# Wide row-sum products, transposes by DMA and a new instruction order in a fused attention and rational-activation MLP kernel

## The chip, the cores and the metric

The kernel runs on one core of a Trainium2 chip. The metric is the device time of one execution in microseconds (us). Times are medians of several runs. Every group of runs also holds runs of the kernel before on the same chip, and a ratio below is the mean time of a kernel's fast runs over the mean time of the fast runs of before in the same rounds, so it is not quite the ratio of the two medians. The interval beside it is a 95% interval. A run more than 1.5% above the fastest run of its kernel counts as slow and is left out of the ratios; the medians and ranges are of all runs. Each profile is of one single run.

## The reference

```
scores = (q @ k^T) / sqrt(64)                  # q, k, v: 8 batches, 8 heads, 576 positions, 64
mask:  heads 0-3: 0 <= i-j < 32                 # local
       heads 4-7: i >= j and i%32 == j%32       # strided
x = softmax(masked scores) @ v                  # rearranged to 4608 x 512
h = x @ w_in                                    # 512 -> 2048
g = (a0 + a1 h + a2 h^2 + a3 h^3) / (1 + |b0||h| + |b1| h^2 + 1e-6)
out = g @ w_out                                 # 2048 -> 512
```

## The kernel before

The work of one batch is attention in five tiles (0 to 3 hold 512 of the positions, tile 4 the remaining 64) and then a chunk of 512 rows of the MLP. Attention of later batches runs between the dense products of earlier chunks. The program is a list of operations, each a group of instructions of one engine with its dependencies, and a list `ORDER` gives each operation its rank in its engine's stream. An operation that has to wait therefore holds up everything behind it on the same engine.

The softmax denominators come from TensorE: each block of 32 columns of exponentials (`ES`, `EW`) is loaded as weights and multiplied once by the values and once more by a column of ones. `psA` is the accumulator; its column 64 in each group of 128 is the denominator.

```python
# attend(), tiles 0-3: strided heads
for h in range(4):
    for g in range(4):
        gh, j = divmod(g, 2); u = 2 * h + gh
        w = ES[es][64*c:64*c+64, j, 64*u+32*sh : 64*u+32*sh+32]           # 64 x 32 weights
        mm(pa4[32*g:32*g+32, 1, h, 0:64],  w, VT[iv][64*c:64*c+64, h, 64*g:64*g+64])
        mm(pa4[32*g:32*g+32, 1, h, 64:65], w, ONE[64*c:64*c+64, :])       # row sums
# tile 4: the same with EW, 128 x 32 weights
...
# VectorE: RC = 1 / psA[.., 64];  XR = psA[.., 0:64] * RC
# SyncE:   XT = DMA transpose of XR  (feeds the first dense product, psH <- XT, Win)
```

Other parts that matter here:

```python
TB, NF0 = 8, 70
# queries and keys of the strided heads, batches b < TB: TensorE transposes into PSUM, VectorE copies to sT
# first-layer weight Win: 4 loads of 0.5 MB early on;  second-layer weight, one load of 2 MB:
def load_wout(key, dep):                       # issued by GpSimd after the loads of batch 2's turn
    add("POOL", lambda e: e.dma_start(Wout[:, :, :], w_out.rearrange("(f p) o -> p f o", p=128)), ...)
# first values: one VectorE, one ScalarE (1.91 us) and one GpSimd (2.6 us) copy into VL
# warm-up: NF0 filler products of 128 columns
```

The softmax here doesn't subtract the row's maximum and nothing guards it: scores larger than these inputs give would overflow.

Of the kernel before, what the change touches and what calls it, by code (L numbers as in the profile page):

```python
# [4 lines left out]
dt = mybir.dt  # L5
Alu = mybir.AluOpType
AF = mybir.ActivationFunctionType
BF = dt.bfloat16
# [7 lines left out]
def _bf16_bits(x):  # L16
# [7 lines left out]
    0, 2, 1, 19, 3, 127, 71, 72, 73, 116, 33, 86, 99, 156, 153, 83, 110, 78, 105, 114, 34, 17, 98, 101, 109,  # L24
    12, 103, 36, 140, 82, 53, 108, 117, 97, 61, 25, 43, 118, 100, 50, 18, 112, 26, 60, 48, 29, 87, 55, 32,
    52, 23, 11, 104, 49, 51, 22, 30, 85, 35, 41, 56, 28, 84, 107, 59, 57, 44, 94, 81, 37, 119, 10, 62, 31,
    115, 111, 21, 141, 42, 15, 46, 45, 14, 40, 66, 79, 4, 27, 6, 58, 7, 68, 5, 38, 9, 13, 16, 8, 20, 24, 92,
    91, 93, 102, 77, 90, 132, 139, 65, 54, 39, 122, 47, 126, 63, 69, 70, 113, 75, 160, 158, 147, 154, 157,
    159, 67, 76, 74, 80, 64, 89, 88, 96, 95, 106, 123, 130, 131, 133, 136, 120, 124, 125, 143, 146, 135,
    142, 144, 148, 151, 129, 134, 138, 145, 150, 152, 170, 173, 178, 197, 207, 216, 221, 240, 121, 137, 162,  # L30
    164, 171, 194, 184, 202, 188, 179, 182, 198, 191, 175, 208, 149, 128, 204, 236, 239, 215, 211, 301, 299,
    229, 303, 193, 206, 228, 234, 225, 237, 238, 242, 243, 245, 161, 168, 174, 181, 183, 192, 200, 186, 190,
    195, 196, 203, 210, 155, 163, 165, 166, 169, 213, 232, 172, 176, 189, 217, 231, 241, 177, 187, 167, 180,
    201, 214, 223, 249, 256, 227, 235, 244, 246, 254, 283, 199, 209, 185, 205, 219, 226, 212, 220, 233, 250,
    292, 357, 375, 312, 341, 300, 307, 315, 322, 393, 398, 252, 258, 260, 263, 272, 255, 262, 264, 269, 273,
    265, 270, 274, 278, 280, 257, 268, 277, 281, 285, 230, 267, 275, 302, 287, 324, 333, 337, 343, 224, 222,
    251, 253, 261, 259, 282, 286, 290, 266, 271, 247, 276, 248, 294, 291, 279, 218, 318, 319, 306, 311, 313,
    320, 316, 296, 460, 284, 289, 293, 298, 304, 310, 314, 323, 327, 334, 309, 339, 345, 350, 355, 342, 347,
    348, 354, 353, 359, 360, 363, 365, 369, 370, 374, 373, 376, 378, 380, 381, 389, 390, 400, 288, 295, 297,
    305, 331, 335, 340, 382, 402, 351, 362, 372, 383, 386, 414, 308, 326, 317, 329, 406, 434, 438, 459, 479,  # L40
    448, 468, 494, 498, 514, 518, 330, 371, 356, 366, 377, 388, 384, 395, 410, 418, 426, 436, 503, 472, 521,
    442, 457, 483, 488, 501, 536, 325, 321, 328, 361, 336, 344, 346, 352, 349, 332, 338, 358, 364, 368, 392,
    396, 385, 387, 425, 427, 403, 405, 435, 409, 445, 415, 367, 379, 391, 397, 404, 412, 420, 429, 439, 444,
    394, 421, 451, 466, 464, 449, 452, 453, 458, 461, 463, 465, 469, 470, 473, 475, 478, 477, 480, 482, 484,
    485, 534, 548, 578, 407, 416, 399, 408, 424, 432, 413, 422, 441, 454, 431, 447, 462, 489, 456, 467, 507,
    523, 527, 567, 581, 552, 558, 543, 551, 574, 587, 612, 624, 535, 554, 557, 563, 580, 593, 603, 634, 541,
    549, 555, 559, 562, 615, 597, 599, 608, 568, 576, 590, 598, 604, 701, 669, 703, 670, 411, 428, 401, 455,
    417, 430, 437, 446, 443, 423, 419, 440, 433, 450, 491, 495, 487, 493, 547, 550, 505, 502, 513, 510, 515,
    544, 471, 476, 481, 486, 490, 492, 497, 500, 504, 509, 474, 496, 512, 516, 519, 564, 570, 571, 573, 575,
    577, 579, 611, 583, 589, 591, 594, 595, 600, 601, 605, 606, 655, 660, 693, 506, 511, 517, 528, 532, 546,  # L50
    525, 531, 553, 556, 561, 565, 585, 592, 538, 560, 613, 621, 627, 674, 677, 654, 702, 640, 645, 688, 729,
    713, 734, 635, 656, 663, 675, 694, 709, 717, 744, 609, 618, 628, 643, 662, 672, 762, 691, 668, 667, 679,
    705, 719, 725, 791, 761, 765, 790, 499, 508, 533, 530, 545, 539, 524, 526, 529, 537, 522, 542, 520, 540,
    626, 620, 617, 629, 651, 653, 614, 610, 647, 642, 657, 641, 566, 572, 584, 586, 588, 596, 602, 607, 616,
    619, 582, 623, 625, 630, 632, 676, 681, 683, 686, 687, 690, 692, 697, 698, 706, 708, 721, 711, 715, 716,
    718, 723, 742, 776, 795, 633, 646, 650, 665, 673, 682, 638, 648, 689, 696, 700, 710, 714, 720, 658, 671,
    724, 732, 737, 803, 814, 788, 810, 752, 758, 775, 825, 830, 838, 750, 769, 778, 797, 807, 827, 832, 856,
    730, 740, 755, 764, 785, 789, 802, 823, 826, 793, 813, 821, 831, 835, 839, 899, 842, 907, 569, 637, 631,
    652, 622, 666, 684, 644, 636, 659, 639, 661, 649, 664, 731, 733, 735, 728, 759, 757, 738, 739, 766, 743,
    774, 771, 678, 685, 695, 699, 704, 707, 712, 722, 727, 745, 726, 749, 753, 770, 772, 784, 792, 794, 798,  # L60
    799, 804, 805, 808, 812, 815, 816, 819, 818, 822, 824, 828, 837, 872, 873, 876, 736, 741, 747, 767, 773,
    781, 780, 796, 786, 800, 806, 820, 829, 833, 801, 809, 836, 844, 848, 888, 912, 879, 901, 864, 866, 921,
    929, 933, 942, 862, 875, 880, 892, 913, 925, 930, 946, 846, 858, 870, 877, 886, 904, 905, 900, 898, 889,
    897, 928, 931, 939, 962, 966, 943, 963, 779, 680, 783, 787, 751, 782, 754, 760, 777, 746, 748, 768, 763,
    756, 852, 847, 841, 843, 874, 868, 855, 850, 861, 857, 863, 859, 811, 817, 834, 845, 851, 854, 867, 878,
    881, 883, 869, 884, 887, 895, 910, 885, 890, 891, 893, 894, 902, 903, 916, 906, 909, 911, 914, 918, 922,
    923, 926, 964, 983, 985, 994, 840, 849, 853, 860, 865, 871, 915, 919, 882, 896, 908, 917, 920, 927, 924,
    932, 935, 938, 941, 965, 974, 953, 976, 949, 951, 968, 998, 993, 1002, 947, 954, 957, 969, 973, 979,
    986, 1006, 944, 948, 950, 952, 958, 992, 991, 997, 961, 970, 972, 977, 980, 984, 1015, 987, 1012, 988,
    934, 937, 940, 945, 955, 960, 936, 956, 967, 971, 975, 978, 982, 990, 959, 981, 995, 1000, 1001, 1034,  # L70
    1043, 1020, 1039, 1013, 1017, 1051, 1060, 1026, 1037, 1007, 1021, 1023, 1030, 1036, 1041, 1046, 1067,
    989, 996, 999, 1003, 1005, 1011, 1014, 1009, 1008, 1016, 1019, 1022, 1025, 1028, 1054, 1029, 1033, 1056,
    1004, 1018, 1027, 1032, 1042, 1045, 1010, 1024, 1050, 1055, 1058, 1074, 1085, 1081, 1095, 1062, 1064,
    1080, 1091, 1096, 1100, 1048, 1059, 1065, 1071, 1076, 1082, 1084, 1099, 1110, 1087, 1088, 1105, 1108,
    1112, 1121, 1089, 1093, 1098, 1103, 1104, 1106, 1119, 1113, 1116, 1118, 1130, 1143, 1145, 1035, 1047,
    1094, 1127, 1133, 1137, 1142, 1136, 1139, 1141, 1146, 1148, 1150, 1031, 1038, 1040, 1044, 1049, 1053,
    1073, 1072, 1075, 1052, 1057, 1061, 1063, 1066, 1068, 1077, 1079, 1069, 1070, 1078, 1083, 1086, 1090,
    1124, 1123, 1135, 1126, 1092, 1097, 1101, 1102, 1115, 1132, 1131, 1128, 1120, 1107, 1109, 1111, 1114,
    1117, 1122, 1125, 1129, 1134, 1138, 1140, 1144, 1147, 1149, 1151, 1152, 1153, 1159, 1157, 1156, 1155,
    1154, 1158, 1160, 1162, 1161  # L80
# [203 lines left out]
def bass_strided_sparse_attn__then__act_rational_pade_kernel(nc, q, k, v, moe_w_in, moe_w_out, moe_a, moe_b, out):  # L284
    w_in, w_out, pa, pb = moe_w_in, moe_w_out, moe_a, moe_b
    B, H, S, D = q.shape
# [10 lines left out]
    HL, DA, TB, NF0 = 4, 1, 8, 70  # L297
# [18 lines left out]
    ES = [A(f"ES{i}", [128, 2, 512], BF) for i in range(NE)]  # L316
    EL = [A(f"EL{i}", [128, 2, 512], BF) for i in range(NE)]
    EX = [A(f"EX{i}", [128, 2, 64], BF) for i in range(NE)]
    EW = [A(f"EW{i}", [128, 12, 2, 32], BF) for i in range(NE)]
# [72 lines left out]
    def cload(name, dst_t, arr, key):  # L392
        g = chan(name).group()
        c = const(name + "_v", arr)
        return add("SP", (lambda e: e.dma_start(dst_t.bitcast(dt.uint16)[:, :], c[:, :])), [], 0.1, key, g, 0.1)
# [6 lines left out]
    cst_c = nc.inline_tensor(cst_np, name="c_cst")  # L402
    cons = []
    cons.append(add("SP", lambda e: e.dma_start(
        cst[:, :], bass.AP(tensor=cst_c, offset=0, ap=[[0, 128], [1, 2]])), [], 0.1, -500, gC, 0.1))
    cons.append(add("SP", lambda e: e.dma_start(
        coef[:, 0:4], bass.AP(tensor=pa.tensor, offset=pa.offset, ap=[[0, 128], [1, 4]])), [], 0.1, -500, gC, 0.1))
    cons.append(add("SP", lambda e: e.dma_start(
# [740 lines left out]
```

## Time and profile before

Before the change the kernel takes 382.73 us (median of 3; 382.16 to 1815.88, the last being the very first execution). The profiled execution has a span of 381.5 us.

In the profiles PE and PEld are TensorE's products and weight loads, DVE is VectorE, ACT ScalarE, POOL GpSimd and SP SyncE. "Issue" is time in which an engine waited for nothing that the profile shows. The granted clock is the share of TensorE's full clock that the chip allowed.

The profile page of before: the span, each engine's busy time with its share and its instructions, TensorE's busy tenths and its granted clock in tenths over 40 equal slices, and the chain of waits followed back from the end, by engine and by line.

```profile
span 381.5 us, 10809 instructions
PE 335.1 (88%) x4902; PEld 178.3 (47%) x4902; DVE 320.0 (84%) x280; ACT 286.9 (75%) x234; POOL 136.0 (36%) x193
PE   4859948989983699999999999999999999999940
PEclk9967975999996699999999999999999999999995
PE 74%; DMA 8%; DVE 7%; issue 4%; ACT 3%; SPq 1%; DVEq 0%
```

The row of tenths shows two halves. Up to slice 14 (about 128 us) TensorE has holes, and its clock is at times halved; after that it reads 9 until the last two slices. The clock matters for time: eight 128x512 products take 3.42 us where it is halved and 1.73 us elsewhere. The table by stretches (start:end, length, then busy us and instructions of PE, PEld, DVE, ACT and POOL, then granted clock, DMA share, GB/s) says the same in numbers.

```profile
100.00:120.00 20.00, 15.50 (x451) 9.40 (x449) 18.27 (x20) 14.81 (x14) 9.18 (x13) 0.95 1.09 129
120.00:140.00 20.00, 13.67 (x199) 6.55 (x198) 14.32 (x12) 12.78 (x12) 16.75 (x24) 0.71 1.33 161
140.00:200.00 60.00, 60.00 (x944) 30.64 (x942) 56.38 (x39) 53.43 (x42) 19.27 (x25) 1.00 0.60 85
```

The worst hole, at 113 to 128 us, seems to have an owner. The first lines below are the view of the tile `Wout` (its load by GpSimd is issued at 107.3 us and takes 19.0 us to land); the last is from the chain of waits in order of time (start, length, what).

```profile
L460 POOL DMA_DIRECT2D Wout<-in_moe_w_out_dram x1: 1180/1180/1180, 107.3 to 107.3; - x1
DMA to landing us min/median/max: 19.0/19.0/19.0
115.75 12.59 DMA XT<-XR
```

A transpose of 128 KB that the next dense chunk needs takes 12.6 us to land while the weight is being loaded (the median of all such transposes in this trace is 4.1 us). The weight lands at 107.3 + 19.0 = 126.3 us, the transpose at 128.3, and the dense chunk starts at 128.4 us. The view of waits puts only 2.1 us of TensorE's own idle time here directly on `XT`, more on "issue" (3.0) and on other engines.

How cheap are the row sums? The groups by form for tile `psA` list duration of one matmul in ns (min/median/max), the first and last start, and the shape of the array piece.

```profile
L597 PE MATMUL psA<-ONE,ES x432: 161/164/188, 21.2 to 261.8; 64*32 64x1 bf16 x144
L597 PE MATMUL psA<-VT,ES x416: 186/197/239, 21.1 to 261.8; 64*32 64x64 bf16 x139
```

Each is 0.16 to 0.20 us from start to end, but products on different 64x32 pieces of the array overlap, as the timeline of one tile shows (start, length of the stretch, what, count; lines left out at the dots):

```profile
161.49 0.24 PE L597 MATMUL psA<-VL,EL 64*32 64x65 bf16 x8
161.54 0.20 PE L597 MATMUL psA<-VT,ES 64*32 64x64 bf16 x1
...
161.62 0.16 PE L597 MATMUL psA<-ONE,ES 64*32 64x1 bf16 x1
161.63 0.20 PE L597 MATMUL psA<-VT,ES 64*32 64x64 bf16 x2
161.64 0.16 PE L597 MATMUL psA<-ONE,ES 64*32 64x1 bf16 x1
...
161.84 0.20 PE L597 MATMUL psA<-ONE,ES 64*32 64x1 bf16 x3
161.97 1.90 PE L597 MATMUL psO<-Wout,T 128*128 128x512 bf16 x8
```

A whole tile of 48 matmuls takes 161.97 - 161.49 = 0.48 us (tile 4: 0.88 us). The 48 start within 0.38 us of each other, 8 ns apart on average (single ones 1 to 28 ns); the last 0.10 us is the change to the next shape. A duration in the list above is a latency, not a cost.

### The profile page before, as it was taken

The page shows a single profiled execution, that of the slowest core. Times are in us where ns is not written, and L with a number is a line of the kernel's source. Part 1 is how long each engine was busy: PE and PEld are TensorE (multiplying, and loading weights), DVE is VectorE, ACT ScalarE, POOL GpSimd, SP SyncE. Part 2 cuts the span into 40 slices and gives each one's busy share as a digit, 9 for nine tenths or more (in the row PEclk, how much of TensorE's full clock was granted, in tenths as well). Part 3 has the DMA queues.
Part 4 walks back from the last instruction along what each step waited for, and adds up shares of the span by engine and source line. Part 5 has one row for each costly group of instructions (what it writes and reads, how often), then busy time and mean ns, then how long its engine had stood idle before and what let it go on. Part 6 is the DMA issues. An engine that isn't in the chain of part 4 may idle for free.

```text
span 381.5 us, 10809 instructions
## 1 busy us (share of the span) xinstructions
PE 335.1 (88%) x4902; PEld 178.3 (47%) x4902; DVE 320.0 (84%) x280; ACT 286.9 (75%) x234; POOL 136.0 (36%) x193
## 2 busy tenths in 40 slices
PE   4859948989983699999999999999999999999940
PEld 4734536554452345554555455454444455544410
DVE  0545995979989588899999999999999999999930
ACT  2423891889983598979889999799998899877710
POOL 0893898706934930069308802600000000000000
PEclk9967975999996699999999999999999999999995
DMA  6999999849999960689839694915020331140412
GB/s 206 194 183 166 94 151 99 96 68 85 153 109 179 173 83 2 77 115 127 140 81 93 110 142 88 106 25 125 15 47 9 76 82 29 41 97 1 103 30 87
DMA packets 80254, 37.10 MB, mean 97 GB/s; under 512 B 49360, under 2 KB 75152, under 8 KB 80208
## 3 DMA queue, kind: packets, MB, share of 16 engines
q0 software_dynamic: 48576, 16.79, 41.1%
q1 hardware_dynamic: 31632, 19.62, 24.8%
q8 instruction: 38, 0.62, 0.7%
q14 instruction: 8, 0.07, 0.1%
HBM read 36.90 MB, written 9.44 MB: 121 GB/s over the span
## 4 chain that ended last, share of the span: by engine, by line
PE 74%; DMA 8%; DVE 7%; issue 4%; ACT 3%; SPq 1%; DVEq 0%
PE psO L597 33%; PE psH L597 21%; PE psS L597 10%; PE psA L597 7%; DMA XT<-XR 3%; DMA XW<-XR 2%; DMA HB<-in_k_dram 2%; PE psS L600 2%; DVE XR L855 2%; DVE UU L976 1%; DVE T L1002 1%; ACT HB L947 1%; DVE UU L973 1%; DVE T L961 1%; DVE T L1012 1%
## 5 line engine op out<-in xcount | busy, mean ns | idle before, releaser
L597 PE MATMUL psO<-Wout,T 128*128 128x512 bf16 x512 | 116.8, 379 | 0.0
L597 PE MATMUL psH<-XT,Win 128*128 128x512 bf16 x336 | 82.2, 387 | 2.6 <-DMA XT<-XR 2.1
L985 ACT ACTIVATE UU<-UU,cst 128x2048 bf16<-128x2048 bf16 (+1 forms) x38 | 72.3, 1910 | 4.4 <-DVE UU L976 4.4
L597 PEld LDWEIGHTS psO<-Wout,T 128*128 128x128 bf16 x512 | 48.8, 98 | 55.8
L988 ACT ACTIVATE UU<-UU 128x2048 bf16<-128x2048 bf16 (+1 forms) x38 | 68.5, 1819 | 0.1
L947 ACT ACTIVATE HB<-psH 128x1024 bf16<-128x1024 f32 x48 | 49.1, 1023 | 20.4 <-PE psH L597 20.1
L597 PEld LDWEIGHTS psH<-XT,Win 128*128 128x128 bf16 x336 | 31.3, 99 | 40.7 <-issue 3.7
L1012 DVE TENSOR_TENSOR T<-T,UU 128x4096 bf16<-128x4096 bf16 (+2 forms) x23 | 41.9, 1821 | 6.0 <-ACT UU L988 5.5
L499 POOL DMA_DIRECT2D VL<-in_v_dram x24 | 24.1, 1010 | 55.8 <-PE psA L597 55.8
L976 DVE TENSOR_TENSOR UU<-UU,T 128x4096 bf16<-128x4096 bf16 (+2 forms) x23 | 42.0, 1827 | 0.6
L1002 DVE TENSOR_TENSOR T<-T,HB 128x8192 bf16<-128x8192 bf16 (+3 forms) x17 | 41.0, 2412 | 0.3
L1006 DVE TENSOR_TENSOR T<-T,HB 128x8192 bf16<-128x8192 bf16 (+3 forms) x17 | 41.0, 2412 | 0.3
L961 DVE TENSOR_SCALAR T<-HB 128x8192 uint16<-128x8192 uint16 (+3 forms) x17 | 22.1, 1305 | 5.4 <-ACT HB L947 4.3
L973 DVE TENSOR_SCALAR UU<-T,coef 128x4096 bf16<-128x4096 bf16 (+2 forms) x23 | 25.8, 1122 | 0.7
L597 PE MATMUL psO<-XT,Win 128*128 128x512 bf16 x96 | 24.4, 399 | 1.0 <-DVE XT L608 0.5
L855 DVE TENSOR_TENSOR XR<-psA,RC 128x512 bf16<-128x512 f32 (+1 forms) x35 | 22.0, 630 | 2.1 <-DMA XW<-XR 0.8
L1009 DVE TENSOR_SCALAR T<-T,coef 128x8192 bf16<-128x8192 bf16 (+3 forms) x17 | 23.2, 1367 | 0.2
L478 POOL DMA_DIRECT2D tm<-in_k_dram x32 | 20.3, 638 | 8.6 <-DMA HB<-in_q_dram 8.6
L1004 DVE TENSOR_SCALAR T<-T,coef 128x8192 bf16<-128x8192 bf16 (+3 forms) x17 | 22.9, 1345 | 0.3
L995 ACT ACTIVATE T<-HB,coef 128x4096 bf16<-128x4096 bf16 x6 | 22.8, 3794 | 0.0
L1078 ACT ACTIVATE OS<-psO 128x1024 f32<-128x1024 f32 x16 | 16.5, 1030 | 8.0 <-PE psO L597 7.9
L478 POOL DMA_DIRECT2D tm<-in_q_dram x32 | 22.1, 695 | 0.3 <-DMA LT<-tm 0.3
(165 smaller groups left out, 501.3 us busy)
## 6 DMA issues: line engine op xcount, KB each, us to landing
out_dram<-OS SPq DMA_DIRECT2D x72, 128.0 KB
kn<-in_k_dram POOLq DMA_DIRECT2D x14, 256.0 KB, 5.7
qn<-in_q_dram POOLq DMA_DIRECT2D x14, 256.0 KB, 5.3
Win<-in_moe_w_in_dram POOLq DMA_DIRECT2D x4, 512.0 KB, 7.6
Wout<-in_moe_w_out_dram POOLq DMA_DIRECT2D x1, 2048.0 KB, 19.0
VL<-in_v_dram POOLq DMA_DIRECT2D x24, 72.0 KB, 3.8
VT<-in_v_dram POOLq DMA_DIRECT2D x12, 128.0 KB, 4.3
HB<-in_k_dram SPq DMA_DIRECT2D x2, 512.0 KB, 6.7
```

Of the source, the lines that this page charges most:

```text
L478: add("POOL", (lambda e, h=h, r0=r0: e.dma_start(tm[r0:r0 + 16, :].rearrange("x (g y d) -> x y g d", g=4, y=2)[:, h % 2], src[b, h, 512:57 ...
L597: return lambda e: e.matmul(out_ap, l, r, start=start, stop=stop, skip_group_check=True)
L855: o3 = add("DVE", (lambda d, rc=rc, x=x, src=src, nh_=nh_: d.tensor_tensor(x[:, 0:64 * nh_].rearrange("x (h d) -> x h d", h=nh_), src[:, : ...
L947: o2 = add("ACT", (lambda a, hb=hb, ps=ps, f=f: a.activation(hb[:, f:f + 2, :], ps[:, :, :], AF.Copy)), [o1, old], ca(1024), key.of("HB"))
L961: d1 = add("DVE", (lambda d, hb=hb, t3=t3, g_=g_: d.tensor_scalar(t3.bitcast(dt.uint16)[:, g_, :], hb.bitcast(dt.uint16)[:, g_, :], 0x7FFF ...
L973: d2 = add("DVE", (lambda d, u=u, t3=t3, sl=sl, HG=HG: d.tensor_scalar(u[:, 0:HG, :], t3[:, sl, :], b1_ap, b0_ap, op0=Alu.mult, op1=Alu.add)),
L976: d3 = add("DVE", (lambda d, u=u, t3=t3, sl=sl, HG=HG: d.tensor_tensor(u[:, 0:HG, :], u[:, 0:HG, :], t3[:, sl, :], op=Alu.mult)), [d2], ct ...
L985: ln = add("ACT", (lambda a, u=u, zl=zl: a.activation(u[:, zl, :], u[:, zl, :], AF.Ln, bias=cst[:, 0:1], scale=1.0)), [d3, cons], 0.28 + w ...
L988: ex.append(add("ACT", (lambda a, u=u, zl=zl: a.activation(u[:, zl, :], u[:, zl, :], AF.Exp, scale=-1.0)), [ln], 0.21 + w * 0.000833, kz + ...
L1002: d5 = add("DVE", (lambda d, hb=hb, t3=t3, g_=g_: d.tensor_tensor(t3[:, g_, :], t3[:, g_, :], hb[:, g_, :], op=Alu.mult)), [d4], ctt(n), k ...
L1006: d7 = add("DVE", (lambda d, hb=hb, t3=t3, g_=g_: d.tensor_tensor(t3[:, g_, :], t3[:, g_, :], hb[:, g_, :], op=Alu.mult)), [d6], ctt(n), k ...
L1012: d9 = add("DVE", (lambda d, t3=t3, u=u, sl=sl, HG=HG: d.tensor_tensor(t3[:, sl, :], t3[:, sl, :], u[:, 0:HG, :], op=Alu.mult)), [d8, ex], ...
```

## The change

Its intent is fewer instructions and fewer stalls. (1) `ES` and `EW` are laid out so that the weights of four (tile 4: two) neighbouring blocks are contiguous, and one ones product with 64x128 (128x64) weights replaces four (two) narrow ones. (2) The query and key transposes of batches 4 to 7 become DMA transposes (`TB` 8 to 4). (3) The first values reach two of their three places by DMA. (4) 20 fillers of 512 columns replace 70 of 128. (5) A new `ORDER`. The diff, cut to its core (the order list, cost numbers that only a scheduler outside the kernel read, and repetitions are left out):

```diff
-    HL, DA, TB, NF0 = 4, 1, 8, 70
+    HL, DA, TB, NF0 = 4, 1, 4, 20
-    ES = [A(f"ES{i}", [128, 2, 512], BF) for i in range(NE)]
+    ES = [A(f"ES{i}", [128, 2, 8, 2, 32], BF) for i in range(NE)]
-    EW = [A(f"EW{i}", [128, 12, 2, 32], BF) for i in range(NE)]
+    EW = [A(f"EW{i}", [128, 2, 12, 32], BF) for i in range(NE)]
...
-        for eng, o0, i0, n in (("DVE", 64, 64, 64), ("ACT", 32, 64, 32)): ...
-        evl.append(add("POOL", (lambda e: e.tensor_copy(VL[0][0:32, 1:8, :, 0:64], stv[96:128, 0:7, :, :])), ...
+        evl.append(evac("DVE", VL[0][64:128, 0:8, :, 0:64], stv[64:128, :, :, :], ...
+        add("SP", (lambda e: e.dma_start(VL[0][32:64, 0:8, :, :], VL[0][64:96, 0:8, :, :])), ...
+        add("SP", (lambda e: e.dma_start(VL[0][0:32, 1:8, :, :], VL[0][96:128, 0:7, :, :])), ...
...
     for g in range(4):                                       # tiles 0-3
-        w = ES[es][64 * c:64 * c + 64, j, 64 * u + 32 * sh:64 * u + 32 * sh + 32]
+        w = ES[es][64 * c:64 * c + 64, sh, u, j, :]
         makers.append(mm(pa4[32 * g:32 * g + 32, 1, h, 0:64], w, VT...))
-        makers.append(mm(pa4[32 * g:32 * g + 32, 1, h, 64:65], w, ONE[64 * c:64 * c + 64, :], False, True))
+    makers.append(mm(pa4[:, 1, h, 64:65],
+                     ES[es][64 * c:64 * c + 64, sh, 2 * h:2 * h + 2, :, :].rearrange("x g j q -> x (g j q)"),
+                     ONE[64 * c:64 * c + 64, :], False, True))
...                                                           # tile 4: one of 128x64 for two of 128x32
```

## The prediction

> **What bounds the kernel now.** The chain of waits is 74% TensorE; DMA is 8%, "issue" 4%. The table by stretches shows two phases. From 128 us on TensorE is full (20.0 of every 20 us, granted clock 1.00); the starts of consecutive matmuls in the timeline leave about 1 us of gaps in 238 us (eight 128x512 matmuls take 1.73 us). VectorE is nearly as full (19.0 to 19.8 of 20). Before 128 us TensorE loses about 23 us in gaps over 0.6 us: about 10 us at 113-128 us, where XT transposes (12.6 us in the chain) queue behind the 2 MB Wout load issued at 107 us, and about 8 us of "issue" stalls at 22-25 and 52-61 us in runs of small matmuls, both at half clock.
>
> **What the change does, costed from the trace.**
>
> 1. Ones products: 16 become 4 in tiles 0-3, 16 become 8 in tile 4, per batch. A weighted-value tile takes 0.48 us for 48 matmuls (161.49 to 161.97 us), 8 ns each, because 64x32 pieces of the array overlap. So 12 fewer save at most 0.1 us a tile. But the new ones products use another array shape (64x128 among 64x32; 128x64 among 128x32). The Trainium skill, "TensorEngine Tiling (Array Packing)", Key Properties, says that changing tiling mode drains the TensorE. This trace agrees: every change of shape costs 91 to 97 ns beyond the streaming time (64x32 to 64x64 94 ns, 128x32 to 64x32 94 ns, 128x128 to 128x64 91 ns), column-only changes included. The new code changes shape 7 more times in tiles 0-3 and 15 more in tile 4. Estimate: 0.12 us into each ones product, 0.1 us out; 0.48 becomes about 1.0 us, tile 4 0.88 becomes about 2.1 us; 3.3 to 3.7 us more per batch, 26 to 30 us in all.
> 2. From batch 4 on the q/k transposes leave TensorE (1.0 us each) and VectorE (1.21 us copy) for four DMA transposes (now 3.3 to 4.5 us to landing): -4 us TensorE, -5 us VectorE.
> 3. First values: a 1.91 us ScalarE copy and a 2.6 us GpSimd copy become two DMAs (now 3.7 to 5.3 us to landing): about neutral.
> 4. Fillers: 20 of 512 columns for 70 of 128: about neutral.
> 5. Order: the Wout load is followed by three or four dense groups before the next first-layer chunk instead of one, recovering perhaps 5 us of the stall; small matmuls are more spread and about 450 fewer, so most issue stalls should go.
>
> **On the critical path.** After 128 us TensorE has no slack: tiles of batches 4 to 7 add about 16 us, three transposes remove 3: +13 us. Before 128 us, +13 us of drains stand against about 5 (Wout), 5 to 8 (issue) and 1 (transpose): about -3 to +3 us, the part I know least.
>
> **Predicted: 392 us, 376 to 404.** Faster by over 2%: 0.17; within 2%: 0.28; slower by over 2%: 0.55.
>
> **What would show it.** Right: gaps of about 0.1 us around every ones product, tile spans near 1.0 and 2 us; TensorE still full in the second half, but longer; VectorE share falling to about 80%; "issue" and the XT transpose shrinking in the chain. Wrong: tile spans at or below 0.48 us.
>
> **What would make it wrong.** If 64x32 to 64x128 needs no drain, step 1 gains about 3 us, and with steps 2 and 5 the time falls to some 368 us. If the new order recovers most of the early gaps, the drains are just paid for and the time stays near 383. If DMA transposes are late under load, it is worse.

## The result, and the profile after

The changed kernel takes 407.4 us (403.81 to 410.34, 4 runs, one of them slow); before in the same job, 383.01 us (the median of four, that very first run included). The ratio is 1.061 (1.051 to 1.072): slower, as predicted, but by 24.4 us where 9.3 were predicted, and outside the range.

The same lines of the page, after:

```profile
span 401.9 us, 9689 instructions
PE 361.3 (90%) x4340; PEld 190.1 (47%) x4340; DVE 314.7 (78%) x276; ACT 285.7 (71%) x233; POOL 130.6 (33%) x192
PE   1789999899982989999999999999999999999950
PEclk9967998999997899999999999999999999999985
PE 72%; DVE 13%; DMA 6%; SPq 2%; ACT 2%; issue 1%; DVEq 0%
```

There are 562 fewer matmuls, yet TensorE is busy 26.2 us longer. "Issue" fell from 4% of the chain to 1%, and the first half has fewer holes. The clock is no excuse: it is higher than before (0.955 against 0.936 over the span). The time of an attention tile tells where the busy time comes from. The timeline of one tile in the second half (start, length of the stretch, what, count):

```profile
168.41 0.24 PE L595 MATMUL psA<-VL,EL 64*32 64x65 bf16 x8
168.47 0.21 PE L595 MATMUL psA<-VT,ES 64*32 64x64 bf16 x2
168.49 0.23 PE L595 MATMUL psA<-VL,EL 64*32 64x65 bf16 x8
168.56 0.19 PE L595 MATMUL psA<-VT,ES 64*32 64x64 bf16 x2
168.68 0.17 PE L595 MATMUL psA<-ONE,ES 64*128 64x1 bf16 x1
168.78 0.21 PE L595 MATMUL psA<-VT,ES 64*32 64x64 bf16 x4
168.93 0.17 PE L595 MATMUL psA<-ONE,ES 64*128 64x1 bf16 x1
169.03 0.21 PE L595 MATMUL psA<-VT,ES 64*32 64x64 bf16 x4
169.17 0.17 PE L595 MATMUL psA<-ONE,ES 64*128 64x1 bf16 x1
169.28 0.21 PE L595 MATMUL psA<-VT,ES 64*32 64x64 bf16 x4
169.42 0.17 PE L595 MATMUL psA<-ONE,ES 64*128 64x1 bf16 x1
169.53 1.90 PE L595 MATMUL psO<-Wout,T 128*128 128x512 bf16 x8
```

Read the first column: each 64x128 product starts about 0.12 us after the last 64x32 one, and the next 64x32 one starts 0.10 us after it. The tile takes 169.53 - 168.41 = 1.12 us (most tiles 1.11) where it took 0.48. Over the whole trace, start to start, the 128 changes from 64x32 to 64x128 take at least 119 ns (median 132), the 100 changes back 104 ns (median), and around the 128x64 products of tile 4 it is 133 and 121 ns. Before, two 64x32 neighbours were 8 ns apart on average. The trace of before has 137 such changes of shape, the trace of after 489. Tile 4 went from 0.88 to 2.42 us, so one batch costs 4 x 0.63 + 1.54 = 4.06 us more of TensorE.

VectorE sees it too: it now waits for TensorE's tiles. The view of waits for VectorE, before and then after (us in total, times, longest):

```profile
DVE RC L853 <- PE psA L597: 7.1, 9, 1.3
```
```profile
DVE RC L856 <- PE psA L595: 24.2, 23, 2.9
```

The stall behind the weight load is still there, with the same signature as before: its load is issued at 111.0 us, lands 18.0 us later, and the dense chunk waits.

```profile
L457 POOL DMA_DIRECT2D Wout<-in_moe_w_out_dram x1: 1222/1222/1222, 111.0 to 111.0; - x1
DMA to landing us min/median/max: 18.0/18.0/18.0
118.57 11.15 DMA XT<-XR
```

To compare kernels, I split every profile at the first dense product of the fourth chunk, the one that this stall delays. "First part" is the time to that product, "second part" is from there to the start of the last matmul.

| profile | first part | second part | sum |
|---|---|---|---|
| before | 128.4 | 238.0 | 366.4 |
| after | 129.8 | 257.0 | 386.8 |

The sum differs by 20.4 us, like the spans of these two runs. (After's profiled run was its fastest, which is why the medians lie 24 apart.) The first part is 1.4 us longer, the second 19.0 us.

How far can such a split be trusted? The kernel a_narrow below was profiled twice: its parts are 121.1 and 242.0 us in one profile, 125.3 and 243.3 in the other. The mean granted clock of the first part was 0.94 in the one and 0.90 in the other. So one profile's first part can be 4 us off, and a difference of 1 or 2 us between two profiles shows nothing. The new order also ran its first part at a higher clock than before (before 0.87, after 0.92); how much of the first part's time is clock was not separated.

### The profile page after: what moved, and what is told of

Same layout as the page of the kernel before. It is cut to its first block, busy times and chain, and to the rows that moved or that the text cites. A ratio compares the mean times of both kernels' runs of the same rounds, so it can differ in the third digit from the quotient of the medians.

```text
span 401.9 us, 9689 instructions
## 1 busy us (share of the span) xinstructions
PE 361.3 (90%) x4340; PEld 190.1 (47%) x4340; DVE 314.7 (78%) x276; ACT 285.7 (71%) x233; POOL 130.6 (33%) x192
## 4 chain that ended last, share of the span: by engine, by line
PE 72%; DVE 13%; DMA 6%; SPq 2%; ACT 2%; issue 1%; DVEq 0%
PE psO L595 25%; PE psH L595 18%; PE psA L595 15%; PE psS L595 11%; DMA XT<-XR 3%; DVE UU L979 2%; PE psS L598 2%; DMA T<-in_v_dram 2%; DVE T L1009 2%; DVE T L1005 2%; DVE T L1015 2%; DMA VL<-VL 2%; DVE UU L976 1%; DVE T L964 1%; DVE T L1002 1%
## 5 line engine op out<-in xcount | busy, mean ns | idle before, releaser
L595 PEld LDWEIGHTS psH<-XT,Win 128*128 128x128 bf16 x336 | 30.3, 97 | 44.4 <-DMA XT<-XR 7.8
L496 POOL DMA_DIRECT2D VL<-in_v_dram x24 | 19.7, 828 | 38.1 <-PE psA L595 37.5
L475 POOL DMA_DIRECT2D tm<-in_k_dram x32 | 23.9, 754 | 12.8 <-DMA HB<-in_q_dram 12.8
L856 DVE RECIPROCAL RC<-psA 128x8 f32<-128x8 f32 (+1 forms) x35 | 6.9, 197 | 24.2 <-PE psA L595 24.2
L595 PE MATMUL psO<-XT,Win 128*128 128x512 bf16 x96 | 24.4, 398 | 0.7 <-DVE T L418 0.7
L475 POOL DMA_DIRECT2D tm<-in_q_dram x32 | 20.9, 671 | 12.1 <-DMA LT<-tm 12.1
L595 PE MATMUL psA<-VT,ES 64*32 64x64 bf16 x416 | 23.8, 199 | 0.0
```

The costliest lines, as they stand in the source:

```text
L475: add("POOL", (lambda e, h=h, r0=r0: e.dma_start(tm[r0:r0 + 16, :].rearrange("x (g y d) -> x y g d", g=4, y=2)[:, h % 2], src[b, h, 512:57 ...
L595: return lambda e: e.matmul(out_ap, l, r, start=start, stop=stop, skip_group_check=True)
```

## The experiments

Theory: the row-sum products cost their changes of shape, and that is the whole loss. Rivals: the wide product is slow in itself; the new layout slows its neighbours; or other parts of the change lose time. A second question soon proved the harder one: the prediction had counted on about 15 us of gains from everything else. Where are they?

### 1. Undoing or isolating one part

`a_narrow` is the changed kernel with narrow ones products (on the new layout, with all else changed):

```diff
+        makers.append(mm(pa4[32 * g:32 * g + 32, 1, h, 64:65], w, ONE[64 * c:64 * c + 64, :], False, True))
-    makers.append(mm(pa4[:, 1, h, 64:65], ES[...four blocks...], ONE[64 * c:64 * c + 64, :], False, True))
```

> The changed kernel with the ones products narrow again (16 per tile, 64x32 and 128x32), everything else of the change kept. Theory D (shape changes drain the array): tile spans return from 1.11 to 0.48 us and from 2.42 to 0.88 us for tile 4, TensorE loses 4.06 us per batch, 17.8 us of it after the first dense chunk of batch 3 where it is full; the time falls from about 406 to 375-386 us. Rival O (the new order, DMA transposes and first-value DMAs are to blame, the drains hide in waits): it stays at or above 400 us although the tiles shrink.

`b_wide` is the opposite: the kernel before with the new layout and the wide products only.

> The kernel before with only the relaid tiles and wide ones products, its own order, transposes, fillers and first values. Theory D: tile spans 1.11 and 2.42 us, time 383 + 16 to 32 = 399 to 415 us. Rival O: at most 388 us.

`a_group` is the changed kernel with its wide products moved behind all other products of the tile, which leaves one change of shape where there were seven or more:

```diff
     for h in range(4):
         for g in range(4):
             makers.append(mm(pa4[32*g:32*g+32, 1, h, 0:64], w, VT...))
-        makers.append(mm(pa4[:, 1, h, 64:65], ES[...], ONE...))
+    for h in range(4):
+        makers.append(mm(pa4[:, 1, h, 64:65], ES[...], ONE...))
```

> The changed kernel with the same wide ones products, all issued after the tile's last 32-column product, so one change of shape into them instead of four (tile 4: eight). Theory D: about 0.55-0.65 us a tile and 1.0-1.1 us for tile 4, time within 5 us of a_narrow. Rival W (a wide product is itself slow, for its 128-column weight load): tile spans stay above 0.9 us and the time near 400 us.

`a_oldfirst` is the changed kernel with the old ScalarE and GpSimd copies of the first values.

> The changed kernel with the first values copied by ScalarE and GpSimd as before instead of by two DMAs. If the DMAs' 6 us to landing on the chain cost what the trace suggests, the first attention tile starts about 2.5 us earlier and the time falls by 1 to 3 us, to about 404; if they are neutral, as predicted, the time is unchanged within 1 us.

| kernel | median us (range) | ratio (interval) | shape changes |
|---|---|---|---|
| before, same rounds | 382.73 | 1 | 137 |
| a_narrow | 383.45 (380.15 to 388.19) | 1.000 (0.994 to 1.006) | 141 |
| b_wide | 403.26 (401.04 to 405.3) | 1.054 (1.049 to 1.060) | 485 |
| a_group | 380.5 (377.22 to 383.02) | 0.992 (0.985 to 0.999) | 185 |
| a_oldfirst | 408.59 (407.62 to 409.63) | 1.068 (1.063 to 1.073) | |

One of the four runs of a_narrow and one of a_group were slow and are not in the ratios. What theory D expected of a_narrow and b_wide came true; a_oldfirst did not fall to 404.

The ones products alone cost 20.5 us in before's surroundings (b_wide against before) and 24 us in the changed ones (after, which ran in another job, against a_narrow). The same number of wide products, grouped, costs nothing that the time shows: in the trace of `a_group`, this tile takes 0.53 us, and four wide products share a quarter of a microsecond.

```profile
154.52 0.24 PE L595 MATMUL psA<-VL,EL 64*32 64x65 bf16 x8
154.57 0.21 PE L595 MATMUL psA<-VT,ES 64*32 64x64 bf16 x2
...
154.64 0.30 PE L595 MATMUL psA<-VT,ES 64*32 64x64 bf16 x12
154.87 0.25 PE L595 MATMUL psA<-ONE,ES 64*128 64x1 bf16 x4
155.05 0.39 PE L595 MATMUL psO<-Wout,T 128*128 128x512 bf16 x1
```

So it is neither the wide product (they start about 25 ns apart here) nor the layout (a_narrow keeps it): it is alternating shapes. Nor is it that two products want the same piece of the array: before, each ones product used the piece of the values product ahead of it, and neighbours started 8 ns apart on average. The first values are neutral or a little better by DMA (a_oldfirst 408.59, after 407.4 in another job, so 1 us is not told apart). But `a_narrow` shows that the rest of the change, taken together, is worth nothing: 383.45 against 382.73 us.

The split into two parts explains a little. In its profile the first part is 121.1 us (7.3 shorter than before), the second 242.0 (4.0 longer); in the second profile of the same kernel it is 3.1 shorter and 5.3 longer. In the first of the two, about 2.4 us of small products had moved from the first to the second part, about 2 us of new short waits came there (3.1 against 0.9), 1.2 us more for the same dense products, and 7 more changes of shape; against that stand about 3 us of transposes that TensorE no longer does.

### 2. The transposes, the weight load, and no ones products at all

`a_group_pe` is a_group with TensorE and VectorE transposing the queries and keys of all batches again (`TB` = 8; the ranks of the added operations are mine).

> a_group with the q/k transposes of batches 4 to 7 back on TensorE with a VectorE copy, one dense group kept between each transpose and its first user. If the DMA transposes give what was predicted (TensorE 1.0 us and VectorE 1.2 us per batch, TensorE having no slack in the second half), this is 3 to 5 us slower than a_group (ratio to before about 1.001 to 1.006). Rival Q: the DMA transposes come late behind other DMAs and give the gain back as waits; then it is equal to a_group or faster.

`a_group_wl` is a_group with the 2 MB load split in four and held back until the last of tiles 0 to 3 of batch 3 is normalised:

```diff
-        add("POOL", e.dma_start(Wout[:, :, :], w_out...), dep, ...)
+        for z in range(4):
+            add("POOL", e.dma_start(Wout[:, 4*z:4*z+4, :], w_out...[:, 4*z:4*z+4, :]), dep + [last tile's XR], ...)
```

> a_group with the 2 MB second-layer weight load cut into four loads that start only when the last attention tile of batch 3 is normalised, so that the XT transposes of batch 3 are no longer queued behind it. If the queueing is what stalls TensorE for 8 us at 111-119 us and halves its clock for 7 us after, the gap shrinks to under 3 us and the time falls by 5 to 9 us against a_group (ratio about 0.97 to 0.98). Rival: the stall moves to the first use of the second-layer weights, and the time is unchanged.

`a_v128` is the changed kernel without any ones product. Each 32-column product of the strided heads streams 128 columns, 64 of values and 64 of ones, so the denominators come along in the same instruction:

```diff
-        makers.append(mm(pa4[32*g:32*g+32, 1, h, 0:64], w, VT[iv][64*c:64*c+64, h, 64*g:64*g+64], h == 0, True))
-    makers.append(mm(pa4[:, 1, h, 64:65], ES[...], ONE[64*c:64*c+64, :], False, True))
+        makers.append(mm(pa4[32*g:32*g+32, 1, h, 0:128], w, values_and_ones(iv, 64*c, 64, h, g), h == 0, True))
```

> The changed kernel without any ones product: each 32-column value product streams 128 columns, 64 of V and 64 of ones, so the denominators come with it. No extra shape changes at all and 12 (tile 4: 8) fewer matmuls. Theory D: a tile takes 0.42-0.50 us, tile 4 0.85-1.0 us, so time at or 2 to 4 us below a_group. If streaming twice the columns binds instead, tiles are 0.6 us and more.

`a_v128_wl` has both edits.

> a_v128 and the late, split weight load together. If both work and are independent, 7 to 12 us below a_group, about 368 to 373 us, faster than both kernels of the case.

| kernel | median us (range) | ratio (interval) |
|---|---|---|
| before, same rounds | 383.54 | 1 |
| a_group_pe | 381.65 (380.39 to 383.43) | 0.996 (0.992 to 1.000) |
| a_group_wl | 377.48 (375.04 to 379.76) | 0.984 (0.980 to 0.988) |
| a_v128 | 378.93 (377.64 to 381.52) | 0.989 (0.985 to 0.993) |
| a_v128_wl | 375.79 (375.14 to 376.21) | 0.980 (0.977 to 0.983) |

`a_group_pe` is 0.4% above a_group, with overlapping intervals: the DMA transposes bring about 1.5 us here, if anything, not the 4 us of TensorE that they take away. The waits of TensorE at 100 to 132 us show where the difference went, first in a_group, then in a_group_pe:

```profile
PE psH L595 <- DMA XT<-XR: 7.9, 1, 7.9
```
```profile
PE psH L542 <- DMA XT<-XR: 4.5, 1, 4.5
```

With its transposes done by TensorE the kernel reaches the fourth chunk 4.3 us later, and then waits 3.4 us less. Both start the chunk at nearly the same time, 118.8 and 119.6 us. Something else sets that time.

What it may be can be read off all eight kernels with an early load, from their views of the tile `Wout` and their timelines:

| profile | load issued | load landed | fourth chunk starts |
|---|---|---|---|
| before | 107.3 | 126.3 | 128.4 |
| after | 111.0 | 129.0 | 129.8 |
| a_narrow | 102.4 | 120.2 | 121.1 |
| a_group | 100.6 | 117.9 | 118.8 |
| a_group_pe | 101.3 | 119.1 | 119.6 |
| a_v128 | 101.2 | 119.3 | 119.8 |
| a_oldfirst | 112.5 | 130.9 | 131.6 |
| b_wide | 110.9 | 129.7 | 131.7 |

The chunk starts 0.5 to 2.1 us after the weight has landed, in every one (and 1.0 us after it in the second profile of a_narrow, where the load was issued at 106.8). If the load sets the time, work saved between its issue and this point cannot show. The Trainium skill, "DMA: Bandwidth & Descriptors", section "Issuing engines are not separate DMA queues", says that DMAs started by different engines run on the same 16 DMA engines and interleave. This trace agrees: the load is issued by GpSimd, the transposes by SyncE, and the slower half of the four transposes takes about 9 to 14 us to land in each of these kernels, against 2.3 to 7.6 us in a_v128_wl2 below, where the load is held back.

`a_group_wl` is 0.8% below a_group, with intervals that just overlap, but its profile still has a gap of 7.6 us, which contradicts what I had expected of it. The reason is in its timeline: the load went out at 107.64 us and the last of the four transposes at 108.78, so the load still overtook it: that transpose took 10.0 us to land. I had not held it back far enough. The run does tell two things apart: the chunk started at 118.8 us, as in a_group, so splitting the load and issuing it 7 us later moved nothing by itself; and it started 6 us before the last quarter of the weight had landed (124.9), so it is the transpose that the chunk waits for, not the weight.

`a_v128_wl` missed its expectation too (368 to 373 us; 375.79 measured). In its profile the first part is 6.7 us shorter than in a_v128 (113.0 against 119.8), but the second 5.0 longer (245.5 against 240.5), with a new wait of 4.1 us of TensorE for a DMA transpose of keys.

### 3. Holding the load back until the transposes have landed

`b_wl2` is the kernel before with this one edit: four loads of 0.5 MB, each depending on the landing of all four `XT` transposes of batch 3. With it go a later place of the loads in GpSimd's stream (rank 484 instead of 460) and second-layer products that wait for their own quarter only; these were not tried apart.

> The kernel before, with one thing changed: the 2 MB second weight is loaded in four pieces of 0.5 MB, and none is issued until all the DMA transposes that feed the fourth block of dense products (XT of batch 3) have landed. Before, the load is issued at 107.3 us and the transposes behind it take 12.6 us to land, with 10 us of TensorE gaps at 113 to 128. Theory A (the load is what holds the transposes up, and the prediction was right that some 5 us can be won there): the transposes land within about 4 us, the gap goes, 377 to 380 us, ratio 0.985 to 0.992. Theory B (the gap is only where slack shows, and VectorE or the small transfers set the pace of both halves): the transposes still take over 8 us, or the gap goes and the time stays within 1 us of before, ratio 0.997 to 1.003.

`a_narrow_wl2` was to be a_narrow with the same edit. By a mistake of mine the unedited file of a_narrow was sent. Its expectation describes a kernel that was not run there:

> The changed kernel with narrow ones products again (383.45 us before this edit) and the same late, split weight load as in b_wl2: nothing of it is issued before the four XT transposes of batch 3 have landed. In a_narrow the stall was 5.9 us at 115.2. Theory A (the load causes the stall and the stall is worth its length): 378 to 380 us, ratio about 0.987 to 0.992. Theory B (the stall is slack of another limit): 382.5 to 384.5 us, ratio 0.998 to 1.003. With b_wl2 it also says what the rest of the change (four DMA transposes, first values by DMA, filler, order) is worth once neither kernel stalls there: if a_narrow_wl2 and b_wl2 agree within 2 us, it is nothing.

| kernel | median us (range) | ratio (interval) |
|---|---|---|
| before, same rounds | 383.04 | 1 |
| b_wl2 | 376.54 (374.64 to 383.96) | 0.980 (0.976 to 0.984) |
| a_narrow again | 384.97 (382.67 to 389.72) | 1.001 (0.997 to 1.006) |

Theory A of b_wl2 holds, with a gain a little above its range (376.54 us where it said 377 to 380): this edit to the kernel before is worth about 2%. Two of its six runs were slow (383.59 and 383.96 us), and the profile fell in such a run, so no line of it is used as evidence. The mistaken run is still useful (one of its six runs was slow): it repeats that a_narrow equals before. Its profile has the same wait for `XT` (4.2 us).

### 4. Is the rest of the change worth nothing once the stall is gone?

For these runs, the late load is the edit of b_wl2 in all four.

> The run that the label a_narrow_wl2 was meant to be (by an error the file of a_narrow was sent there, so that run only repeats a_narrow: 384.97 us, ratio 1.0014). Here the changed kernel has narrow ones products and the second weight is loaded in four pieces, none issued before the four XT transposes of batch 3 have landed. In b_wl2 the same edit took the kernel before from 383.0 to 376.5 us (ratio 0.98). Theory A (the rest of the change saves nothing that the weight load does not hide): the edit is worth the same here, 376 to 378 us, ratio 0.98 to 0.987, level with b_wl2. Theory B (the changed order had already used part of that stall): 380 to 383 us, ratio 0.992 to 1.0, so slower than b_wl2. Theory C (the stall hid gains of the rest): below 374 us.

> The kernel before with two edits and nothing of the change: the late split weight load of b_wl2, and no ones products at all (the 32-column products of the remote keys stream 128 columns, 64 of values and 64 of ones, as a_v128 does). a_v128 took 1.1% off a_narrow by the same edit. If the two gains add: 372 to 374 us, ratio 0.97 to 0.976. If the ones products cost nothing here because VectorE sets the pace of phase 1 in this kernel (84% busy against 78%): 375.5 to 377 us, as b_wl2.

> a_v128_wl (375.79 us, ratio 0.98) with its weight load held back further: until the XT transposes of batch 3 have landed, instead of until one tile's rows are written. In a_v128_wl gaps of 1.8 and 4.3 us were left at 111 to 120 us, and the load was still issued in the same microsecond as the last transpose. If the load is what is left of the stall: 371 to 374 us, ratio 0.968 to 0.975. If what is left is the DMA transposes of the queries and keys of batch 4 that stand in the same queue (they took 10 us in its chain of waits): 375 to 377 us, no better.

> a_v128_wl2 with the queries and keys of batches 4 to 7 transposed by TensorE and copied by VectorE again, as the kernel before does, so the DMA transposes are gone from the queue in which the XT transposes stand. If those DMA transposes hold up XT: faster than a_v128_wl2 by 2 us or more. If they do not, slower by the 1 to 2 us that a_group_pe lay above a_group, or the same within 1 us.

| kernel | median us (range) | ratio (interval) | first part | second part |
|---|---|---|---|---|
| before, same rounds | 382.44 | 1 | (128.4) | (238.0) |
| a_narrow_wl3 | 377.37 (374.86 to 379.63) | 0.983 (0.977 to 0.989) | 119.7 | 241.6 |
| b_v128_wl2 | 373.62 (368.58 to 375.37) | 0.971 (0.964 to 0.978) | 119.5 | 236.9 |
| a_v128_wl2 | 370.25 (369.96 to 373.52) | 0.967 (0.962 to 0.972) | 115.8 | 240.2 |
| a_v128_pe_wl2 | 377.39 (375.92 to 379.57) | 0.985 (0.980 to 0.990) | 116.8 | 243.0 |

(The parts of before are those of its one profile. Two of the six runs of b_v128_wl2 count as slow and are not in its ratio, since they lie over 1.5% above its fastest; their clock was no lower, and with them its ratio would be 0.974. The profile of a_v128_wl2 is of its slowest run, 373.52 us; the other five took 369.96 to 370.70.) In the trace of a_v128_wl2, the last `XT` transpose is issued at 111.86 us and the load follows it at 114.44 us; the transposes took 2.3 to 7.6 us to land, and no wait of TensorE for `XT` is left at 100 to 132 us.

```profile
111.86 1.19 SPq L841 DMA_TRANSPOSE XT<-XR  x1
114.44 3.78 POOL L415 DMA_DIRECT2D Wout<-in_moe_w_out_dram  x4 [11.02 <-DMA XT<-XR]
```

What follows:

- a_narrow_wl3 (0.983) and b_wl2 (0.980) are level, as theory A had it. Without the stall as with it, the rest of the change (transposes, first values, filler, order) sums to nothing measurable. b_v128_wl2 and a_v128_wl2 ask it again and differ by 0.3%, with overlapping intervals. Their parts suggest how: in these two profiles the changed order has a first part shorter by 3.7 us and a second part longer by 3.3 us. It would then move time from one part to the other, as in both profiles of a_narrow (7.3 and 3.1 shorter, 4.0 and 5.3 longer); single profiles do not show it more firmly.
- The DMA transposes inside it are worth something, though. a_v128_pe_wl2 is 7 us slower than a_v128_wl2, more than the run expected, and the intervals do not overlap; between the two profiles it is 3.8 us (1.0 and 2.8), since that of a_v128_wl2 is of its slowest run. While the stall was there, they showed as about 1.5 us. So the 4 us that were expected of them seem to be there, and since the whole sums to nothing, something else in the new order must then cost about as much. Which operations of the order these are, I have not separated; and since the place of the TensorE transposes in that order is my choice, the 7 us may contain some of it.
- Dropping the ones products altogether saves 1.6% over the narrow ones in the changed order (a_narrow_wl3 to a_v128_wl2). In the order of before it is 0.9% at most (b_wl2 to b_v128_wl2, in different jobs, with overlapping intervals), so not shown there. Why is not settled: the tile takes 0.46 us against 0.48, which does not sum to 3 us or more.
- a_v128_wl2 beats both kernels: 370.25 us, 3.3% below before and 9% below after.

## Why the prediction was right or wrong

- *Step 1, the drains of shape changes (a drain is the wait at such a change): right in mechanism and nearly in size.* It put 3.3 to 3.7 us on a batch; 4.06 were measured. Tile spans of 1.0 and 2.1 us were predicted, 1.12 and 2.42 measured. The changes around 64x128 and 128x64 take 104 to 133 ns start to start, a little over the 91 to 97 ns beyond streaming that the prediction read from before's shapes. In the time of the kernel 20.5 to 24 us appeared of the predicted 26 to 30.
- *The step that failed is "On the critical path": the gains set against the drains.* It put 5 us (the weight load), 5 to 8 us (issue) and 1 us into the first part and 3 us of transposes into the second, some 15 us in all. a_narrow measured their sum: 0 within some 2 us (ratio 1.000, 0.994 to 1.006, and 1.001 when repeated). For the second part it said "+13 us"; it was +19.0. The ones products account for 15.0 of that (257.0 - 242.0), close to the 16 predicted. The other +4.0 (+5.3 by the second profile of a_narrow) stands where -3 was written.
- *"Order: recovering perhaps 5 us of the stall": wrong.* The stall does not shrink because more dense work follows the load. The chunk starts when the transposes that share the DMA engines with the load have landed, which in all eight kernels is just after the load has, 17 to 19 us after its issue. The way to the gain was another one: b_wl2 won 6.5 us by holding the load back, and needed nothing of the change for it.
- *"Three transposes remove 3 us": right or a little small, but hidden.* It shows as 3.8 us between two profiles, and 7 us in the medians, once the stall is out; with the stall, 3.4 us came back as a longer wait.
- *"After 128 us TensorE has no slack": right for before, but taken as a promise.* The second part is as long as TensorE's work only as long as the order keeps it fed and the same work stays there. The new order put 2.4 us more work there, and new waits.
- *The first part: predicted -3 to +3, measured +1.4.* It is right only as a sum, so partly by luck: the ones products cost 8.7 us there (129.8 - 121.1) where 13 were written, and the rest of the change gave 7.3 back where 11 to 14 were written (4.5 and 3.1 by the second profile of a_narrow).
- *The number.* The text's own sum was +13 us after 128 us and about 0 before, so 396, but it wrote 392; that the faster cases of its last paragraph pulled it down is a guess. Against 396 the miss is 11 us: about 6 in the second part, 1.4 in the first, and about 4 because the profiled run was the fastest of after's.
- *What it said would show in the profile came true:* gaps of 0.1 us around each ones product, a full TensorE in a longer second half, VectorE's share down (84% to 78%), "issue" down (4% to 1%). The `XT` transpose did not shrink, 12.6 to 11.2 us. First values by DMA were neutral, as it said.

## What to carry to other kernels

Count the changes of array shape on TensorE, not its instructions: taking 16 of 48 products out of a tile saved 0.02 us here (a_v128), and a change of shape added cost about 0.1 us, so group products of one shape or let the row sum ride along as more streamed columns. Before crediting a saving ahead of a stall, find out what ends the stall: if it is a transfer with its own start time, try moving that transfer, since savings beside it may only lengthen the wait. And when one half of a kernel gets shorter by a new order, look at the other half in the same profile before adding the gains, and at a second profile of the same kernel before trusting a few us.

## What the Trainium skill lacked or had wrong

- "TensorEngine Tiling (Array Packing)", Key Properties, says that changing the tiling mode drains TensorE, without a figure. Here a change costs 91 to 97 ns beyond the streaming time among the shapes of before, and 104 to 133 ns start to start around 64x128 and 128x64. It lists 128x32 and 128x64 as different configurations but does not say outright that a change of columns alone counts; here 128x32 to 128x64 costs as much as any (133 ns).
- The same page, Instruction Overhead, gives about 60 cycles of overhead for each matmul and the same latency to one column as to 60. As a cost per instruction this does not fit tiled products: 64x32 neighbours, with 1 as with 64 columns, start 8 ns apart on average (48 in 0.38 us); at the 25 ns that the next point cites, 48 would take 1.2 us. The latencies are 164 ns for one column and 197 for 64, in records whose ends are modelled, so this half is not decided.
- "TensorE: Matmul & The Clock Gate", section "Wait — 56ns, not 53.3ns?", says that start to start never drops below about 25 ns. For four 64x128 products in a row a_group agrees (25 ns). For 64x32 products on different pieces of the array "never" is too strong (8 ns on average); the same page's part on packing small matmuls allows for that, with about 4 ns from one tile to the next.
- "DMA: Bandwidth & Descriptors", section "Queues, rings and completion order", has each DMA engine go round the queues packet by packet. It has no figure for how long a small transpose waits beside a large load. Here the last of the four `XT` transposes landed within 2.1 us of the end of a 2 MB load in all eight kernels with an early load, and single ones took up to 14 us; in a_v128_wl2, with the load held back, they took 2.3 to 7.6 us.
